# Attention with value products of three key tiles per visit, and each group's output projection added up by DVE in the next group

## The chip, the cores and the metric

The kernel runs on one core of a Trainium2 chip. The metric is device time in microseconds, the median of several executions. One execution was also recorded by the hardware profiler; the numbers of engines and single instructions come from it.

The engines have short names here: PE multiplies matrices (PEld is its loading of weights, which runs beside it), ACT computes functions such as the exponential, DVE and POOL work elementwise, SP issues most transfers (DMA). Each engine runs its own instructions in order. PE writes its results to PSUM, a memory of eight banks; a bank holds one result of 128x512 floats.

## The reference, cut to what matters

One sequence of 2048 tokens with 448 features goes through two branches, attention `a` and a mixer with a channel MLP `b`, and a gate `g` mixes them. The change concerns the attention alone: 16 heads of 28 features share one set of keys and values.

```python
q = (x @ wq).reshape(B, S, H, Dh).transpose(0, 2, 1, 3)     # S 2048, H 16, Dh 28
k = x @ wk
v = x @ wv
scores = einsum("bhqd,bkd->bhqk", q, k) * (Dh ** -0.5)
p = softmax(scores, axis=-1)
o = einsum("bhqk,bkd->bhqd", p, v)
a = o.transpose(0, 2, 1, 3).reshape(B, S, H * Dh) @ wo
...
return g * a + (1 - g) * b
```

## The kernel before

The first 424 us compute keys, values and the whole branch `b`, which ends in `x1`, 16 tiles of 128 tokens. The change leaves them alone. The attention stage follows, from line 454 on.

**Groups and key tiles.** Queries are taken in NB = 4 blocks of 512 tokens, heads in NG = 4 sets of four. A pair of a block and a set is a group `u`, 16 in all, and `b, g = divmod(u, 4)`. A group goes over 16 key tiles `kt` of 128 keys, so the main loop (line 646) counts `k` from 0 to 257, two steps (LAG) past the last of 256 key tiles.

**One step of the loop.** For each of four heads PE multiplies a key tile with 512 queries into a score tile `s` (L663), and ACT writes its exponential into a tile `p` (L665). Score tiles go round through five PSUM banks in order (`s_tile`, line 478): two of tag "mm", one of "misc", two of "s". The last group uses three of them; the "s" banks and both "m" banks then hold four output projections that stay open over the group.

**Visits.** At every PVB-th step (line 676) PE turns to value products: `pv_group` (line 618) multiplies the `p` tiles of a key tile with the values into the bank `pv` of the group (L625). With PVB = 2 a visit handles two key tiles, those of two and three steps before, 8 products of two instructions each. The four heads write four partition ranges of the bank and run side by side. The values carry a column of ones, so that row 0 of each range gets the softmax sums. Tag "mx" has one bank: the next group's `pv` takes it when the former has been copied.

**The end of a group.** After the last key tile `recip_begin` (line 523) copies `pv` to SBUF on ACT (`o`, L525), brings the sums into another layout by a transfer (`rt`), takes reciprocals on DVE and sends them back in two parts (`rb`). `norm_job` (line 541) spreads them with one matmul (`rbc`, L543), DVE multiplies, and POOL splits the result into a rounded part `onh` and a rest `onl`.

**Jobs.** Other matmuls are put between the scores. `jobs` is a list of generators, and `pump()` (line 601) runs one to its next yield, which is one matmul for the most part. It is called after the second and the fourth score of each step; in the last group after each. In the list come: `q_job(u + 2)` (from `kt` 2 on, 11 matmuls L503, then ACT and DVE split the result), the `norm_job` of the former group, and, once a block is complete, four `wo_job` (line 567), one for each tile of 128 tokens: 12 matmuls (L556, L558, L560) over the four sets of heads accumulate in one bank, `gate_out` scales them by the gate and adds `x1` on DVE (L564), and a transfer writes the tile out. The last block's sets 0 to 2 are done as jobs in the last group, the fourth in the tail.

**Maxima.** At the end of steps `kt` 6 to 9 four small matmuls (`m`, L166) and a reduction on DVE (L167) find row maxima for the next group; at `kt` 11 they are transposed (`mt`, L193) and copied by ACT (`mrow`, L195). The tiles `q`, `rbc`, `m`, `mt` and `wo` all share the two banks of tag "m". An instruction that wants a bank waits until its last reader is done, and on PE everything behind it waits too: PE's order is the order in which the code writes it.

**Tail.** After the loop the last group's result is transposed, divided, split and projected tile by tile (`tail_a`, `tail_b`, `tail_c`).

Of the kernel before, what the change touches and what calls it, by code (L numbers as in the profile page):

```python
# [8 lines left out]
F32 = mybir.dt.float32  # L9
F32R = mybir.dt.float32r  # L10
AF = mybir.ActivationFunctionType
ALU = mybir.AluOpType
# [3 lines left out]
P = 128  # L16
S = 2048
D = 448
# [4 lines left out]
NB = S // 512  # L23
NT = S // P
NF = F // P
NG = H // 4
# [1 line left out]
EPS = 1e-5  # L28
SHIFTS = (-1, 1, -2, 2)
LAG = 2  # L30
PVB = 2
MK = 128
LIMIT = 1e12

# [1 line left out]
def f32(ap):  # L36
    return ap.bitcast(F32)
# [3 lines left out]
def gated_mix_kernel(  # L41
# [13 lines left out]
    nc = tc.nc  # L55
# [11 lines left out]
    x1 = keep.tile([P, NT, D], F32, name="x1")  # L67
# [3 lines left out]
    gg = keep.tile([P, NT], F32, name="gg")  # L71
# [20 lines left out]
    def misc_tile(name):  # L92
        return psA.tile([P, 512], F32, tag="misc", bufs=1, name=name)
# [59 lines left out]
    NU = NB * NG  # L153
# [4 lines left out]
    def max_tile(name):  # L158
        return psA.tile([P, 512], F32, tag="mx", bufs=1, name=name)
# [294 lines left out]
    with tc.tile_pool(name="s3", bufs=1, reuse_waits="tile") as s3, \  # L454
# [8 lines left out]
        woh = s3.tile([P, 4, D], F32R, name="woh")  # L463
# [11 lines left out]
        def s_spare(name):  # L475
            return psA.tile([P, 512], F32, tag="misc", bufs=1, name=name)

        def s_tile(n, last=False):
            return (mm_tile, mm_tile, s_spare, s_more, s_more)[n % (3 if last else 5)](f"s_{n}")

        xact = {}

# [31 lines left out]
        on_of = {}  # L514
# [24 lines left out]
            return o, rb  # L539

        def norm_job(u, o, rb):
            ps = (mm_tile if u == NU - 2 else misc_tile)(f"rbc_{u}")
            nc.tensor.matmul(ps, sel8, rb, start=True, stop=True)  # L543
            on = s3.tile([P, 512], F32, tag="onf", bufs=2, name=f"on_{u}")
            nc.vector.tensor_mul(on, o, ps)  # L545
            onh = s3.tile([P, 512], F32R, tag="onh", bufs=5, name=f"onh_{u}")
            onl = s3.tile([P, 512], F32R, tag="onl", bufs=5, name=f"onl_{u}")
            nc.gpsimd.tensor_copy(onh, on)  # L548
            nc.gpsimd.tensor_tensor(onl, on, f32(onh), ALU.subtract)
            on_of[u] = (onh, onl)  # L550
            yield

        def wo_group(ps, b, t, g, first, last):
            tok = slice(t * P, (t + 1) * P)
            onh, onl = on_of[b * NG + g]
            nc.tensor.matmul(ps, onh[:, tok], woh[:, g, :], start=first, stop=False)  # L556
            yield
            nc.tensor.matmul(ps, onh[:, tok], wol[:, g, :], start=False, stop=False)  # L558
            yield
            nc.tensor.matmul(ps, onl[:, tok], woh[:, g, :], start=False, stop=last)  # L560

        def gate_out(n, ps):
            ot = s3.tile([P, D], F32, tag="ot", bufs=3, name=f"ot_{n}")
            nc.vector.scalar_tensor_tensor(ot, ps, gg[:, n:n + 1], x1[:, n, :], op0=ALU.mult, op1=ALU.add)  # L564
            nc.sync.dma_start(out[0, n * P:(n + 1) * P, :], ot)

        def wo_job(b, t):
            ps = misc_tile(f"wo_{b}_{t}")[:, 0:D]
            for g in range(NG):
                yield from wo_group(ps, b, t, g, g == 0, g == NG - 1)  # L570
                if g < NG - 1:
                    yield
            gate_out(4 * b + t, ps)
            yield

        wqraw = s3.tile([P, 4, 512], F32, tag="raw", bufs=2, name="wqraw")
        nc.sync.dma_start(wqraw, wq)
# [20 lines left out]
        jobs = []  # L598
# [13 lines left out]
        def drain():  # L612
            while current[0] is not None or jobs:
                pump()
# [3 lines left out]
        def pv_group(k):  # L618
            u, kt = divmod(k, NT)
            if kt == 0:  # L620
                pv_of[u] = max_tile(f"pv_{u}")
            pv = pv_of[u]
            ps = p_of.pop(k)
            for j in range(4):
                nc.tensor.matmul(pv[32 * j:32 * j + 32, :], vext[:, kt, :], ps[j],  # L625
                                 start=(kt == 0), stop=(kt == NT - 1), tile_position=(0, 32 * j))
            if kt == NT - 1 and u < NU - 1:
                o, rb = recip_begin(u, pv_of.pop(u))
                delayed.append((k + 6, lambda: norm_job(u, o, rb)))
                if u == NU - 2:  # L630
                    for t in range(4):
                        delayed.append((k + 10, lambda t=t: wo_last_job(t, NG - 2)))
                elif u % NG == NG - 1:
                    for t in range(4):
                        delayed.append((k + 8, lambda t=t: wo_job(u // NG, t)))

        wo_last = []

        def wo_last_job(t, g):
            if g == 0:  # L640
                wo_last.append((m_tile if t < 2 else s_more)(f"wo_{NB - 1}_{t}")[:, 0:D])
            yield from wo_group(wo_last[t], NB - 1, t, g, g == 0, False)
            yield

        delayed = []
        for k in range(NU * NT + LAG):
            u, kt = divmod(k, NT)
            while delayed and delayed[0][0] <= k:
                jobs.append(delayed.pop(0)[1])
            if k == (NU - 1) * NT:  # L650
                for g in range(NG - 2):
                    for t in range(4):
                        jobs.append(lambda t=t, g=g: wo_last_job(t, g))
            if k < NU * NT:
                if kt == (7 if u == 0 else 2) and u + 2 < NU:
                    jobs.insert(0, lambda u=u: q_job(u + 2))
                if kt == 8 and (u + 3) % NG == 0 and u + 3 < NU:
                    load_x((u + 3) // NG)
                p_of[k] = []
                for j in range(4):  # L660
                    n = 4 * k + j
                    ps = s_tile(n, u == NU - 1)
                    nc.tensor.matmul(ps, kS[0:98, kt * P:(kt + 1) * P], q_of[u][0:98, j, :], start=True, stop=True)  # L663
                    p = s3.tile([P, 512], F32, tag="p", bufs=4 * (LAG + PVB) + 2, name=f"p_{n}")
                    nc.scalar.activation(p, ps, AF.Exp, scale=SCALE)  # L665
                    p_of[k].append(p)
                    if j % 2 == 1 or u == NU - 1:
                        pump()
                if u + 1 < NU:
                    if 6 <= kt < 10:  # L670
                        max_part(u + 1, kt - 6, m_tile)
                    elif kt == 10:
                        max_end(u + 1)
                    elif kt == 11:
                        max_rows(u + 1, m_tile)
            if k >= LAG and k % PVB == PVB - 1:
                for kk in range(k - LAG - PVB + 1, k - LAG + 1):
                    if kk >= 0:
                        pv_group(kk)
        assert not delayed  # L680
        drain()

        u = NU - 1
        pv = pv_of.pop(u)
        o = s3.tile([P, 512], F32, tag="o", bufs=2, name=f"o_{u}")
        onh = s3.tile([P, 512], F32R, tag="onh", bufs=5, name=f"onh_{u}")
        onl = s3.tile([P, 512], F32R, tag="onl", bufs=5, name=f"onl_{u}")
        on_of[u] = (onh, onl)
        toks = [slice(t * P, (t + 1) * P) for t in range(4)]
        on4 = {}  # L690
# [15 lines left out]
            nc.vector.tensor_sub(onl[:, toks[t]], tq, f32(onh)[:, toks[t]])  # L706

        def tail_c(t):
            for _ in wo_group(wo_last[t], NB - 1, t, NG - 1, False, True):
                pass  # L710
            gate_out(4 * (NB - 1) + t, wo_last[t])

        for t in range(4):
            nc.scalar.copy(o[:, toks[t]], pv[:, toks[t]])
# [19 lines left out]
        with tc.If(again > 0):  # L734
            for b in range(NB):
                load_x(b)
                for g in range(NG):
                    u = b * NG + g
                    for _ in q_job(u):
                        pass  # L740
                    max_full(u, m_tile)
                    max_end(u)
                    max_rows(u, m_tile)
                    pv = max_tile(f"pv2_{u}")
                    for kt in range(NT):
# [10 lines left out]
                for t in range(4):  # L756
                    for _ in wo_job(b, t):
                        pass


_OUTS = [((1, S, D), "float32")]
# [48 lines left out]
```

## Time and profile before

| | us |
|---|---|
| median of three runs | 1070.64 (1069.9 to 1074.41) |
| the profiled execution | 1070.98 |
| its span, first to last instruction | 1069.1 |
| first score of the attention stage | 423.9 from the start |
| last group, first score | 1007.5 |
| span of the last value products | 1049.9 to 1053.6 |

The page of a profile lists, for each engine, busy time, share of the span and number of instructions, then the chain of work that ended last, then the costliest groups of instructions. A group's line gives the line of the kernel, engine, operation, what is written and read, the shapes, the count, then the busy time and the mean of one in ns, then idle time of the engine just before them and what ended most of it. Matmuls overlap, so the mean length of one is more than the distance between two.

### The profile page before, as it was taken

The numbers are of one execution on the slowest core, as the hardware profiler recorded it, in microseconds if no ns is written. First come the engines' busy times: TensorE is split into PE (matmuls) and PEld (weight loads), VectorE is DVE, ScalarE is ACT, GpSimd is POOL, SyncE is SP. The second block draws the span as 40 slices with busy tenths as digits, with TensorE's granted clock in tenths as the row PEclk, the third lists the DMA queues.
The fourth block names the chain that finished last, engine by engine and source line by source line (L and its number), as shares of the span: only waits on it lengthen the run. The fifth ranks groups of instructions, "written<-read, shape, count | busy, mean of one in ns | idle before, by whom it ended". The sixth has DMA issues, their size and how long they took to land.

```text
span 1069.1 us, 13948 instructions
## 1 busy us (share of the span) xinstructions
PE 1039.7 (97%) x5610; PEld 679.6 (64%) x5610; DVE 258.0 (24%) x521; ACT 673.2 (63%) x1318; POOL 159.8 (15%) x182
## 2 busy tenths in 40 slices
PE   6999889999999999999999999999999999999995
PEld 4787778888888888454554555554655555555542
DVE  6744952311411311401110110120110210111102
ACT  5444451222222223788888888889888889888873
POOL 5622430110200201603000002010002100000100
PEclk9999899999999999999999999999999999999998
DMA  9401330000000000423211202220202220211001
GB/s 312 131 1 37 111 111 1 1 1 1 1 1 1 1 1 29 164 32 70 33 17 16 31 20 40 39 31 3 39 10 41 39 31 2 40 24 26 10 2 38
DMA packets 30541, 41.15 MB, mean 38 GB/s; under 512 B 8004, under 2 KB 20100, under 8 KB 30340
## 3 DMA queue, kind: packets, MB, share of 16 engines
q1 hardware_dynamic: 30324, 40.04, 16.3%
q8 instruction: 46, 0.75, 0.3%
q14 instruction: 27, 0.22, 0.1%
q10 hardware_dynamic: 144, 0.13, 0.1%
HBM read 23.28 MB, written 3.67 MB: 25 GB/s over the span
## 4 chain that ended last, share of the span: by engine, by line
PE 91%; DVE 4%; DMA 1%; ACT 1%; POOL 1%; issue 1%; SPq 0%; POOLq 0%; ACTq 0%; DVEq 0%
PE s L663 27%; PE pv L625 22%; PE acc L420 4%; PE acc L419 4%; PE acc L421 4%; PE g L115 4%; PE g L116 4%; PE g L117 4%; PE q L503 3%; PE m L166 2%; PE wo L560 1%; PE wo L558 1%; PE wo L556 1%; PE g L119 1%; PE g L118 1%; PE h L116 1%
## 5 line engine op out<-in xcount | busy, mean ns | idle before, releaser
L665 ACT ACTIVATE p<-s 128x512 f32<-128x512 f32 x1024 | 517.6, 627 | 98.1 <-PE s L663 97.8
L663 PE MATMUL s<-qs,kS 98*128 98x512 f32 x1024 | 343.6, 420 | 1.4 <-ACT p L665 0.7
L663 PEld LDWEIGHTS s<-qs,kS 98*128 98x128 f32 x1024 | 181.6, 189 | 168.2 <-ACT p L665 127.1
L625 PE MATMUL pv<-p,vext 128*32 128x512 f32 x2048 | 247.6, 602 | 0.0
L409 ACT ACTIVATE gh<-g 128x512 fp32r<-128x512 f32 x56 | 33.6, 600 | 174.9 <-PE g L119 174.9
L625 PEld LDWEIGHTS pv<-p,vext 128*32 128x32 f32 x2048 | 53.7, 109 | 107.6 <-issue 100.3
L411 DVE TENSOR_TENSOR gl<-gf,gh 128x512 fp32r<-128x512 f32 x56 | 41.3, 738 | 192.1 <-ACT gf L410 192.0
L419 PE MATMUL acc<-w4h,gh 128*128 128x448 f32 x224 | 82.6, 369 | 0.0
L420 PE MATMUL acc<-w4l,gh 128*128 128x448 f32 x224 | 82.0, 366 | 0.0
L421 PE MATMUL acc<-w4h,gl 128*128 128x448 f32 x224 | 81.7, 365 | 0.0
L167 DVE TENSOR_REDUCE mr<-m 128x4 f32<-128x512 f32 x64 | 44.3, 692 | 146.0 <-PE m L166 145.3
L548 POOL CAST onh<-on 128x512 fp32r<-128x512 f32 x15 | 9.2, 614 | 414.8 <-DVE on L545 228.7
L115 PE MATMUL g<-ah,w3h 128*128 128x512 f32 x168 | 67.1, 399 | 3.1 <-ACT gf L410 2.8
L116 PE MATMUL g<-al,w3h 128*128 128x512 f32 x168 | 66.5, 396 | 0.1
L117 PE MATMUL g<-ah,w3l 128*128 128x512 f32 x168 | 66.3, 394 | 0.0
L521 DVE SCALAR_TENSOR_TENSOR good<-rt,good 128x16 f32<-128x16 f32 x15 | 2.6, 175 | 190.2 <-DMA rt<-o 190.2
L419 PEld LDWEIGHTS acc<-w4h,gh 128*128 128x128 f32 x224 | 42.0, 188 | 4.9
L420 PEld LDWEIGHTS acc<-w4l,gh 128*128 128x128 f32 x224 | 42.1, 188 | 4.8
L421 PEld LDWEIGHTS acc<-w4h,gl 128*128 128x128 f32 x224 | 42.0, 188 | 3.6
L166 PEld LDWEIGHTS m<-kS,qs 96*128 96x128 f32 x256 | 38.4, 191 | 6.3 <-DVE mr L167 1.2
L115 PEld LDWEIGHTS g<-ah,w3h 128*128 128x128 f32 x168 | 31.9, 190 | 9.7 <-ACT gf L410 3.3
L564 DVE SCALAR_TENSOR_TENSOR ot<-wo,gg,x 128x448 f32<-128x448 f32 x16 | 10.9, 682 | 108.0 <-PE wo L560 108.0
(204 smaller groups left out, 1144.4 us busy)
## 6 DMA issues: line engine op xcount, KB each, us to landing
qs<-qh SPq DMA_DIRECT2D x32, 256.0 KB
qs<-ql SPq DMA_DIRECT2D x16, 256.0 KB
xq<-in_xT_dram SPq DMA_DIRECT2D x4, 1024.0 KB
x<-in_x_dram SPq DMA_DIRECT2D x4, 896.0 KB
w3raw<-in_w_dram SPq DMA_DIRECT2D x7, 512.0 KB
out_dram<-ot SPq DMA_DIRECT2D x16, 224.0 KB
w4raw<-in_w_dram SPq DMA_DIRECT2D x7, 448.0 KB
xkv<-in_xT_dram SPq DMA_DIRECT2D x3, 1024.0 KB
```

Source lines behind the costliest of these rows:

```text
L115: nc.tensor.matmul(ps, wh[:, c, :], ah[:, c, :], start=(c == 0), stop=False)
L116: nc.tensor.matmul(ps, wh[:, c, :], al[:, c, :], start=False, stop=False)
L117: nc.tensor.matmul(ps, wl[:, c, :], ah[:, c, :], start=False, stop=False)
L166: nc.tensor.matmul(ps[:, j, :], q_of[u][0:96, j, t * P:(t + 1) * P], kS[0:96, 0:MK], start=True, stop=True)
L167: nc.vector.reduce_max(mx_of[u][:, :, t], ps, axis=AX.X)
L411: nc.vector.tensor_sub(gl, gf, f32(gh))
L419: nc.tensor.matmul(ps, gh[:, tok], w4h[i][:, k, :], start=(f == 0), stop=False)
L420: nc.tensor.matmul(ps, gh[:, tok], w4l[i][:, k, :], start=False, stop=False)
L421: nc.tensor.matmul(ps, gl[:, tok], w4h[i][:, k, :], start=False, stop=(f == NF - 1))
L625: nc.tensor.matmul(pv[32 * j:32 * j + 32, :], vext[:, kt, :], ps[j], start=(kt == 0), stop=(kt == NT - 1), tile_position=(0, 32 * j))
L663: nc.tensor.matmul(ps, kS[0:98, kt * P:(kt + 1) * P], q_of[u][0:98, j, :], start=True, stop=True)
L665: nc.scalar.activation(p, ps, AF.Exp, scale=SCALE)
```

## The change

A visit handles three key tiles (PVB = 3). Score tiles rotate through five banks in the last group too. `pump()` is called at six of the twelve scores between two visits, the 5th, 7th, 8th, 10th, 11th and 12th. `norm_job` no longer goes through the list of jobs, but runs at `kt` 7 of the next group as a whole. At `kt` 9 four `wo_job` of that former group join the list: three matmuls each in a bank of their own, and DVE adds the scaled result to `x1` (for the first set of heads) or to the sum so far in `ot` (for the others). After the fourth set the tile is written out. `onh` and `onl` have two buffers instead of five, `ot` five instead of three, and `p` has 22 instead of 18, since the count follows PVB.

```diff
-PVB = 2
+PVB = 3
...
-        def s_tile(n, last=False):
-            return (mm_tile, mm_tile, s_spare, s_more, s_more)[n % (3 if last else 5)](f"s_{n}")
+        def s_tile(n):
+            return (mm_tile, mm_tile, s_spare, s_more, s_more)[n % 5](f"s_{n}")
...
         def norm_job(u, o, rb):
-            ps = (mm_tile if u == NU - 2 else misc_tile)(f"rbc_{u}")
+            ps = misc_tile(f"rbc_{u}")
...
-        def wo_job(b, t):
-            ps = misc_tile(f"wo_{b}_{t}")[:, 0:D]
-            for g in range(NG):
-                yield from wo_group(ps, b, t, g, g == 0, g == NG - 1)
-                if g < NG - 1:
-                    yield
-            gate_out(4 * b + t, ps)
-            yield
+        ot_of = {}
+
+        def wo_job(u, t, tile_of=misc_tile):
+            b, g = divmod(u, NG)
+            n = 4 * b + t
             tok = slice(t * P, (t + 1) * P)
+            onh, onl = on_of[u]
+            ps = tile_of(f"wo_{u}_{t}")[:, 0:D]
+            nc.tensor.matmul(ps, onh[:, tok], woh[:, g, :], start=True, stop=False)
             yield
             nc.tensor.matmul(ps, onh[:, tok], wol[:, g, :], start=False, stop=False)
             yield
+            nc.tensor.matmul(ps, onl[:, tok], woh[:, g, :], start=False, stop=True)
+            before = x1[:, n, :] if g == 0 else ot_of[n]
+            if g == 0:
+                ot_of[n] = s3.tile([P, D], F32, tag="ot", bufs=5, name=f"ot_{n}")
+            nc.vector.scalar_tensor_tensor(ot_of[n], ps, gg[:, n:n + 1], before, op0=ALU.mult, op1=ALU.add)
+            if g == NG - 1:
+                nc.sync.dma_start(out[0, n * P:(n + 1) * P, :], ot_of[n])
...
                 o, rb = recip_begin(u, pv_of.pop(u))
-                delayed.append((k + 6, lambda: norm_job(u, o, rb)))
-                if u == NU - 2:
-                    for t in range(4):
-                        delayed.append((k + 10, lambda t=t: wo_last_job(t, NG - 2)))
-                elif u % NG == NG - 1:
-                    for t in range(4):
-                        delayed.append((k + 8, lambda t=t: wo_job(u // NG, t)))
+                norms.append((u, o, rb))
...
         for k in range(NU * NT + LAG):
             u, kt = divmod(k, NT)
-            while delayed and delayed[0][0] <= k:
-                jobs.append(delayed.pop(0)[1])
-            if k == (NU - 1) * NT:
-                for g in range(NG - 2):
-                    for t in range(4):
-                        jobs.append(lambda t=t, g=g: wo_last_job(t, g))
+            if norms and kt == 7:
+                for _ in norm_job(*norms[0]):
+                    pass
+            if norms and kt == 9:
+                v = norms.pop()[0]
+                for t in range(4):
+                    jobs.append(lambda t=t, v=v: wo_job(v, t))
...
-                    if j % 2 == 1 or u == NU - 1:
+                    if 4 * (k % PVB) + j in (4, 6, 7, 9, 10, 11):
                         pump()
...
         def tail_c(t):
-            for _ in wo_group(wo_last[t], NB - 1, t, NG - 1, False, True):
+            for _ in wo_job(u, t, m_tile if t < 2 else s_more):
                 pass
-            gate_out(4 * (NB - 1) + t, wo_last[t])
```

A branch behind the tail, which recomputes the attention if a softmax sum was too large, calls the changed functions in the same order; it did not run in the profiled execution.

More of the change, by code (lines that the diff above doesn't have):

```diff
@@ L545, in norm_job @@
             nc.vector.tensor_mul(on, o, ps)
-            onh = s3.tile([P, 512], F32R, tag="onh", bufs=5, name=f"onh_{u}")
-            onl = s3.tile([P, 512], F32R, tag="onl", bufs=5, name=f"onl_{u}")
+            onh = s3.tile([P, 512], F32R, tag="onh", bufs=2, name=f"onh_{u}")
+            onl = s3.tile([P, 512], F32R, tag="onl", bufs=2, name=f"onl_{u}")
             nc.gpsimd.tensor_copy(onh, on)
@@ L551, in norm_job @@
             yield
-        def wo_group(ps, b, t, g, first, last):
+        ot_of = {}
+        def wo_job(u, t, tile_of=misc_tile):
+            b, g = divmod(u, NG)
+            n = 4 * b + t
             tok = slice(t * P, (t + 1) * P)
-            onh, onl = on_of[b * NG + g]
-            nc.tensor.matmul(ps, onh[:, tok], woh[:, g, :], start=first, stop=False)
+            onh, onl = on_of[u]
+            ps = tile_of(f"wo_{u}_{t}")[:, 0:D]
+            nc.tensor.matmul(ps, onh[:, tok], woh[:, g, :], start=True, stop=False)
             yield
@@ L559, in wo_group @@
             yield
[L560 to L565, printed above, removed]
-        def wo_job(b, t):
-            ps = misc_tile(f"wo_{b}_{t}")[:, 0:D]
-            for g in range(NG):
-                yield from wo_group(ps, b, t, g, g == 0, g == NG - 1)
-                if g < NG - 1:
-                    yield
-            gate_out(4 * b + t, ps)
-            yield
+            nc.tensor.matmul(ps, onl[:, tok], woh[:, g, :], start=False, stop=True)
[5 more added lines that the diff above has]
+                nc.sync.dma_start(out[0, n * P:(n + 1) * P, :], ot_of[n])
         wqraw = s3.tile([P, 4, 512], F32, tag="raw", bufs=2, name="wqraw")
@@ L628, in pv_group @@
                 o, rb = recip_begin(u, pv_of.pop(u))
-                delayed.append((k + 6, lambda: norm_job(u, o, rb)))
-                if u == NU - 2:
-                    for t in range(4):
-                        delayed.append((k + 10, lambda t=t: wo_last_job(t, NG - 2)))
-                elif u % NG == NG - 1:
-                    for t in range(4):
-                        delayed.append((k + 8, lambda t=t: wo_job(u // NG, t)))
[L637 to L645, printed above, removed]
+                norms.append((u, o, rb))
+        norms = []
         for k in range(NU * NT + LAG):
             u, kt = divmod(k, NT)
-            while delayed and delayed[0][0] <= k:
-                jobs.append(delayed.pop(0)[1])
-            if k == (NU - 1) * NT:
-                for g in range(NG - 2):
-                    for t in range(4):
-                        jobs.append(lambda t=t, g=g: wo_last_job(t, g))
+            if norms and kt == 7:
[5 more added lines that the diff above has]
+                    jobs.append(lambda t=t, v=v: wo_job(v, t))
             if k < NU * NT:
@@ L661, in gated_mix_kernel @@
                     n = 4 * k + j
-                    ps = s_tile(n, u == NU - 1)
+                    ps = s_tile(n)
                     nc.tensor.matmul(ps, kS[0:98, kt * P:(kt + 1) * P], q_of[u][0:98, j, :], start=True, stop=True)
@@ L679, in gated_mix_kernel @@
                         pv_group(kk)
-        assert not delayed
+        assert not norms
         drain()
@@ L685, in gated_mix_kernel @@
         o = s3.tile([P, 512], F32, tag="o", bufs=2, name=f"o_{u}")
-        onh = s3.tile([P, 512], F32R, tag="onh", bufs=5, name=f"onh_{u}")
-        onl = s3.tile([P, 512], F32R, tag="onl", bufs=5, name=f"onl_{u}")
+        onh = s3.tile([P, 512], F32R, tag="onh", bufs=2, name=f"onh_{u}")
+        onl = s3.tile([P, 512], F32R, tag="onl", bufs=2, name=f"onl_{u}")
         on_of[u] = (onh, onl)
@@ L755, in gated_mix_kernel @@
                         pass
-                for t in range(4):
-                    for _ in wo_job(b, t):
-                        pass
+                    for t in range(4):
+                        for _ in wo_job(u, t):
+                            pass
 _OUTS = [((1, S, D), "float32")]
```

## The prediction

> **What bounds the kernel now.** I read the page first: engine times, the chain that ended last, the groups of instructions.
>
> ```profile
> PE 1039.7 (97%) x5610; PEld 679.6 (64%) x5610; DVE 258.0 (24%) x521; ACT 673.2 (63%) x1318; POOL 159.8 (15%) x182
> ...
> PE 91%; DVE 4%; DMA 1%; ACT 1%; POOL 1%; issue 1%; SPq 0%; POOLq 0%; ACTq 0%; DVEq 0%
> ...
> L665 ACT ACTIVATE p<-s 128x512 f32<-128x512 f32 x1024 | 517.6, 627 | 98.1 <-PE s L663 97.8
> ...
> L564 DVE SCALAR_TENSOR_TENSOR ot<-wo,gg,x 128x448 f32<-128x448 f32 x16 | 10.9, 682 | 108.0 <-PE wo L560 108.0
> ```
>
> PE looks full, but that is busy time. The waits, between 462 and 1054 us, say otherwise:
>
> ```profile
> PEld s L663 <- ACT p L665: 118.9, 220, 0.8
> ```
>
> So score matmuls wait on the exponentials, and L665 shows the exponentials waiting on scores: the two run in a loop through the five score banks. Its clockwork is in the timeline. The columns are start, time from the first start to the last end, engine, line, what is written and read, count, idle time before. First a visit with no extra matmuls (all engines; PE, then ACT), then one with four:
>
> ```profile
> 733.87 2.67 PE L663 MATMUL s<-qs,kS 98*128 98x512 f32 x8
> 736.47 1.92 PE L625 MATMUL pv<-p,vext 128*32 128x512 f32 x16
> 738.32 0.73 PE L663 MATMUL s<-qs,kS 98*128 98x512 f32 x2
> ...
> 734.41 4.03 ACT L665 ACTIVATE p<-s 128x512 f32<-128x512 f32 x8 [0.42 <-PE s L663]
> ...
> 735.38 0.60 ACT L665 ACTIVATE p<-s 128x512 f32<-128x512 f32 x1
> ...
> 736.04 0.50 PE L663 MATMUL s<-qs,kS 98*128 98x512 f32 x1
> ```
>
> ```profile
> 703.34 1.92 PE L625 MATMUL pv<-p,vext 128*32 128x512 f32 x16
> 705.19 0.73 PE L663 MATMUL s<-qs,kS 98*128 98x512 f32 x2
> 705.76 0.40 PE L503 MATMUL q<-alq,wqh 128*128 128x512 f32 x1
> 706.00 0.63 PE L663 MATMUL s<-qs,kS 98*128 98x512 f32 x2
> 706.47 0.39 PE L503 MATMUL q<-ahq,wql 128*128 128x512 f32 x1
> ...
> 707.88 0.39 PE L503 MATMUL q<-alq,wqh 128*128 128x512 f32 x1
> 708.20 1.92 PE L625 MATMUL pv<-p,vext 128*32 128x512 f32 x16
> ```
>
> In the plain visit the first score starts at 733.87 and its exponential 0.54 later. The third exponential ends at 735.98, 1.57 after the first began; the eighth score, which needs its bank, starts at 736.04 (+0.06); the value products start 0.43 later and the next score 1.85 after them. 0.54 + 1.57 + 0.06 + 0.43 + 1.85 = 4.45 us: **a loop through the banks**, in which PE and ACT both wait. In the loaded visit PE streams, one matmul every 0.236 us (705.76 to 706.47 holds three); it lasts 4.86 us (703.34 to 708.20). The first score after value products takes 0.335 (0.57 less 0.235), the step into them 0.32, and the way from them to the next score is 1.85, 0.13 over four steps of 0.43 (below): 0.10 + 0.085 + 0.13, one switch costs about 0.31 us.
>
> The bank loop can be tested inside this trace. In the last group scores rotate through three banks, so the eighth waits for the fifth exponential, 2 x 0.49 later (eight end 4.03 after the first starts, three 1.57: 0.49 each). The loop gives 4.45 + 0.98 = 5.43; the chain of waits shows 5.43 from value products to value products, and in the timeline ACT idles 1.41 instead of 0.42:
>
> ```profile
> 1022.14 1.85 PE pv L625 x16
> 1027.57 1.85 PE pv L625 x16
> ```
>
> ```profile
> 1041.44 4.03 ACT L665 ACTIVATE p<-s 128x512 f32<-128x512 f32 x8 [1.41 <-PE s L663]
> ```
>
> **Part 1: three key tiles per visit.** It removes 43 of 129 visits: 43 x 0.31 = 13.3 us if PE alone decided. The Trainium skill says the same in "TensorEngine Tiling (Array Packing)", Tiling Modes, Key Properties: changing the tiling mode drains the TensorE, so fewer changes are fewer drains. The row agrees that a change costs; by this rule alone the kernel gains, and that is a rival below.
>
> But banks stay five while a visit has twelve scores, so the twelfth waits for the *seventh* exponential, which ends 1.57 + 4 x 0.49 = 3.54 after the first begins. The value products are 24 instructions. Their pace:
>
> ```profile
> 1007.54 0.50 PE L663 MATMUL s<-qs,kS 98*128 98x512 f32 x1
> ...
> 1049.91 3.64 PE L625 MATMUL pv<-p,vext 128*32 128x512 f32 x32
> ```
>
> 32 less 16 of them is 3.64 - 1.92 = 1.72 us, 0.43 for each four; so 1.85 + 0.86 = 2.71 to the next score. A plain visit: 0.54 + 3.54 + 0.06 + 0.43 + 2.71 = **7.28 us for three tiles, 2.43 a tile against 2.22**. Five exponentials cover about 2.4 us and no longer reach over the value products: ACT idles some 1.5 us a visit. "Perfetto Trace Analysis", Optimization Strategy, in the Trainium skill, reads a bubble that repeats as a buffer that ran out; the trace agrees, with 1.41 us a visit on three banks.
>
> With all six pump slots filled: the tenth score waits for the fifth exponential, to 0.54 + 2.55 + 0.06 = 3.15; then 0.335, four steps of 0.235 and 0.32 to the value products, 4.75; + 2.71 = 7.46 (PE without waits: 0.335 + 16 x 0.235 + 0.32 + 2.71 = 7.13). That is 2.49 a tile against 2.43.
>
> **Part 2: what falls into a visit's chain.** A group needs 11 q and 12 wo matmuls, in 32 slots. Three groups (48 tiles) are 16 visits; by the slots, ten have a filled last slot: 16 x 7.28 + 10 x 0.18 = 118.3 us. Then:
>
> ```profile
> 711.57 0.56 PE L166 MATMUL m<-kS,qs 96*128 96x128 f32 x4
> ...
> 713.17 0.56 PE L166 MATMUL m<-kS,qs 96*128 96x128 f32 x4
> 713.66 1.92 PE L625 MATMUL pv<-p,vext 128*32 128x512 f32 x16
> ...
> 712.16 0.69 DVE L167 TENSOR_REDUCE mr<-m 128x4 f32<-128x512 f32 x1 [8.40 <-PE m L166]
> ```
>
> The m matmuls at the end of a visit add about 0.4 (0.49 to the value products instead of 0.32, and a step of 0.235), four times in three groups, 1.6; the others, rbc and mt with ACT's mrow mostly hide in bank waits, 1.0 (from 0 if all hide to 2.5 if none). 2.6 together.
>
> **Part 3: the value bank, a new wait.** The tag "mx" has one bank. Sixteen is not a multiple of three, so a visit now holds the last key tile of one group *and* the first of the next in two of three groups (u mod 3 = 0 and 2); the next group's first product must wait for ACT's copy o, and behind it wait all later value products and scores. Before, this boundary fell between visits:
>
> ```profile
> 698.47 1.92 PE L625 MATMUL pv<-p,vext 128*32 128x512 f32 x16
> ...
> 700.46 0.59 ACT L525 COPY o<-pv 128x512 f32<-128x512 f32 x1
> ```
>
> For u mod 3 = 0 the old group's products end 1.92 into the visit, the copy follows 0.07 later and takes 0.59, products resume at about 2.64 instead of 1.72: 0.9. For u mod 3 = 2 the old products end at 1.06, but ACT first finishes its queued exponentials (twelve, 0.48 apart from 0.54 on, to 6.3; the products begin at 4.75), so the copy runs from 1.55 to 2.14; resumed at 2.2 instead of 0.86: 1.3. With 0.2 for the third group's copy, 2.4 per three groups. Bounds: 0 if ACT takes the copy early, 3.4 if every boundary also sees a full copy after idle.
>
> **Part 4: norm_job at kt 7.** It leaves the job queue and asks at once for one of two "m" banks. In groups with u mod 3 = 0 and 1 the pump slots leave q at nine matmuls by then, so q holds one and the m of kt 6 the other. rbc waits for that reduction: m at 711.57, reduction from 712.16 to 712.85, so 1.33 us after m's start instead of 0.40, and every later score of the visit queues behind. By the steps above the twelfth score comes 1.1 and 1.3 late: 2.4 per three groups; nothing if q is done earlier. Where u mod 3 = 2, q is done. The copy lies a whole visit, over 7 us, ahead of rbc; I take rb's small transfers as landed by then.
>
> **Part 5: projections and DVE.** The 192 matmuls stay; 48 more additions of 0.68 us (L564) are 33 us on a DVE that is busy 24%: nothing on the path, except that an "m" bank is held 0.7 us after each wo_job, under the steps to the next (0.1 if not). Output transfers stay 16; with five ot buffers the fifth is free 38 us ahead. p has 22 buffers for 20 live ones, the margin of two as before.
>
> **Sum.** Three groups: 118.3 + 2.6 + 2.4 + 2.4 = 125.7, 41.9 a group. Before, by the copies:
>
> ```profile
> L525 ACT COPY o<-pv x15: 587/587/588, 468.1 to 1013.1; 128x512 f32<-128x512 f32 x15
> ```
>
> (1013.1 - 468.1) / 14 = 38.9. Fourteen groups: +41.6, less 0.6 because u = 14 computes no q. **The last group gains**: five banks, and no saved-up projections. It ran from 1007.54 to 1053.55, 46.0 us. After: three visits of 7.28, two of 7.46, 0.9 for the value bank, then four scores (1.12) and 24 products (2.78): 41.6, so -4.4. The first group and the tail (the same three matmuls and one addition for each t) I take as unchanged. +36.6 in all. The profiled execution took 1071.0 us (span 1069.1), 0.3 above the median of 1070.64; forecast **1108 us**, 3.5% slower.
>
> **The rivals.**
> *The new waits stay away* (parts 3 and 4 cost nothing). For it: the order of ACT's queue isn't in the diff, and a q finished by kt 6 frees its bank. Against: one "mx" bank, two "m" banks. Ten boundaries cost 11.0 and nine norm jobs 11.0: without them 1108 - 22 = 1086 us.
> *The switches decide, faster.* If PE's own stream sets each visit, 43 switches of 0.31 are saved, 13.3, and 4.4 in the last group: 1070.6 - 17.7 = 1053 us. For it: PE at 97%, and loaded visits stream without a wait. Against: the 5.43 us loop of the last group. It decides from the point where a visit's bank chain is about half a microsecond shorter than I have it (37 us over 75 visits); exponentials near 0.41 us apart would do that. The skill's drain rule gives this result, taken alone.
> *The clock drops.* Longer waits on PE at three places in a group could lower its granted clock, as happened once at the start of this stage, where scores ran at ACT's pace:
>
> ```profile
> 424.00:463.60 39.60, 39.11 (x206) 18.82 (x204) 12.50 (x16) 32.57 (x66) 21.75 (x16) 0.96 0.53 150
> 463.60:615.00 151.40, 151.40 (x889) 79.02 (x888) 21.23 (x49) 131.37 (x266) 14.28 (x11) 1.00 0.18 30
> ```
>
> (Busy times of the engines, then the granted clock: 0.96, later 1.00.) 0.04 of 40 us is 1.6; if every second group lost that, and the waits of parts 3 and 4 were half as long again (11), 1108 + 12 + 11 = 1131 us. Against: later waits of up to 0.8 us left it at 1.00.
>
> **Chances.** Forecast 0.65, waits stay away 0.18, switches decide 0.10, clock 0.07. The forecast's own range is 1098 to 1118: part 2's hidden work (5 units of three groups by -1.0 to +1.5) and a few us in the last group. The range 1082 to 1122 takes in the first rival and leaves out the others. Within 0.5%, about what a measurement of this kernel can tell from no change, needs gains and waits to cancel: 0.02. Faster 0.10, slower 0.88.
>
> **What would show it.** Plain visits of 7.28 and loaded ones of 7.46 between starts of value products; ACT idle about 1.5 us before the first exponential of each. Value products waiting on ACT's o at ten boundaries, 0.9 and 1.3 us. rbc waiting on DVE's reduction in nine groups, over 1 us. A last group near 41.6. Visits near 7.1 with no score waiting on p would prove part 1 wrong, and with it the sign.

## The result and the profile after

| | before | changed |
|---|---|---|
| median | 1072.28 us (four runs) | 1117.1 us (1115.56 to 1120.57, four runs) |
| ratio | 1 | 1.0429, interval 1.0407 to 1.0450 |
| profiled execution | 1070.98 us, span 1069.1 | 1118.51 us, span 1116.6 |

The change makes the kernel 4.3% slower. By busy time PE still looks full on the page (96%, 97 before). But PE's share of the chain that ended last has fallen from 91 to 85%, and ACT's has risen from 1 to 5%.

```profile
PE 1072.1 (96%) x5610; PEld 671.7 (60%) x5610; DVE 289.0 (26%) x569; ACT 669.7 (60%) x1318; POOL 159.3 (14%) x182
...
PE 85%; ACT 5%; DVE 5%; POOL 1%; DMA 1%; issue 1%; SPq 0%; ACTq 0%; POOLq 0%
...
L649 ACT ACTIVATE p<-s 128x512 f32<-128x512 f32 x1024 | 514.7, 643 | 147.6 <-PE s L647 147.6
```

The same 1024 exponentials now wait 147.6 us for scores, 98.1 before. PE's waits in the attention stage, between 463 and 1103 us, name what else is new (who waited for whom: total, times, longest):

```profile
PE pv L622 <- ACT o L525: 9.8, 10, 1.4
PE rbc L543 <- DVE mr L167: 7.1, 9, 0.8
PE m L166 <- DVE ql L148: 1.3, 4, 0.3
```

Ten value products wait for the copy of the former group, nine `rbc` for a reduction: the counts that the prediction gave. Two visits without a job, PE and then ACT in the timeline (start, time from first start to last end, engine, line, what is written and read, count, idle time before):

```profile
498.58 2.78 PE L622 MATMUL pv<-p,vext 128*32 128x512 f32 x24
501.29 4.63 PE L647 MATMUL s<-qs,kS 98*128 98x512 f32 x12
505.85 2.78 PE L622 MATMUL pv<-p,vext 128*32 128x512 f32 x24
...
501.83 5.99 ACT L649 ACTIVATE p<-s 128x512 f32<-128x512 f32 x12 [1.53 <-PE s L647]
```

From value products to value products 7.27 us (7.28 predicted), and ACT sits idle for 1.53 before the first exponential. Next, the two kinds of boundary between two groups that fall inside a visit (first u mod 3 = 0, with ACT's copy, then u mod 3 = 2), and a visit in which `rbc` finds both "m" banks taken:

```profile
552.98 1.92 PE L622 MATMUL pv<-p,vext 128*32 128x512 f32 x16
555.61 1.07 PE L622 MATMUL pv<-p,vext 128*32 128x512 f32 x8 [0.70 <-ACT o L525]
...
554.97 0.59 ACT L525 COPY o<-pv 128x512 f32<-128x512 f32 x1 [0.26 <-PE pv L622]
...
769.26 1.06 PE L622 MATMUL pv<-p,vext 128*32 128x512 f32 x8
771.53 1.92 PE L622 MATMUL pv<-p,vext 128*32 128x512 f32 x16 [1.21 <-ACT o L525]
```

```profile
565.20 0.56 PE L166 MATMUL m<-kS,qs 96*128 96x128 f32 x4
566.54 0.50 PE L543 MATMUL rbc<-rb,sel 128*128 128x512 f32 x1 [0.79 <-DVE mr L167]
...
570.15 0.66 PE L166 MATMUL m<-kS,qs 96*128 96x128 f32 x4 [0.34 <-DVE ql L148]
```

In the first the new group's eight products start 2.63 us after the visit's first instead of 1.72: 0.91 late (0.9 predicted). In the second its sixteen start 2.27 after instead of 0.86: 1.41 late (1.3 predicted). `rbc` starts 1.34 after the m matmuls (1.33 predicted). In the last row the third m of that visit waits too, since the bank that q held is not split yet; this one was not predicted.

### The profile page after: what moved, and what is told of

Same layout as the page of the kernel before. It is cut to its first block, busy times and chain, and to the rows that moved or that the text cites. A ratio compares the mean times of both kernels' runs of the same rounds, so it can differ in the third digit from the quotient of the medians.

```text
span 1116.6 us, 14066 instructions
## 1 busy us (share of the span) xinstructions
PE 1072.1 (96%) x5610; PEld 671.7 (60%) x5610; DVE 289.0 (26%) x569; ACT 669.7 (60%) x1318; POOL 159.3 (14%) x182
## 4 chain that ended last, share of the span: by engine, by line
PE 85%; ACT 5%; DVE 5%; POOL 1%; DMA 1%; issue 1%; SPq 0%; ACTq 0%; POOLq 0%
PE s L647 25%; PE pv L622 21%; ACT p L649 4%; PE acc L420 4%; PE acc L419 4%; PE acc L421 4%; PE g L115 3%; PE g L116 3%; PE g L117 3%; PE q L503 3%; PE m L166 2%; PE wo L561 1%; PE g L119 1%; PE g L118 1%; PE wo L565 1%; PE wo L563 1%
## 5 line engine op out<-in xcount | busy, mean ns | idle before, releaser
L649 ACT ACTIVATE p<-s 128x512 f32<-128x512 f32 x1024 | 514.7, 643 | 147.6 <-PE s L647 147.6
L647 PE MATMUL s<-qs,kS 98*128 98x512 f32 x1024 | 368.0, 432 | 0.5
L647 PEld LDWEIGHTS s<-qs,kS 98*128 98x128 f32 x1024 | 184.8, 188 | 181.9 <-ACT p L649 109.1
L622 PEld LDWEIGHTS pv<-p,vext 128*32 128x32 f32 x2048 | 58.0, 111 | 141.3 <-issue 118.7
L569 DVE SCALAR_TENSOR_TENSOR ot<-wo,gg,ot 128x448 f32<-128x448 f32 x48 | 32.7, 683 | 107.0 <-PE wo L565 107.0
L166 PE MATMUL m<-kS,qs 96*128 96x128 f32 x256 | 36.4, 264 | 1.8 <-DVE ql L148 1.3
```

The lines of the kernel that those rows point to most:

```text
L166: nc.tensor.matmul(ps[:, j, :], q_of[u][0:96, j, t * P:(t + 1) * P], kS[0:96, 0:MK], start=True, stop=True)
```

## The experiments

**Four score banks, without and with a second bank for value products.** The chain through the banks was read out of one trace; with one bank less it should get longer by one exponential.

```diff
 def s_more(name):
-    return ps3.tile([P, 512], F32, tag="s", bufs=2, name=name)
+    return ps3.tile([P, 512], F32, tag="s", bufs=1, name=name)
...
-    return (mm_tile, mm_tile, s_spare, s_more, s_more)[n % 5](f"s_{n}")
+    return (mm_tile, mm_tile, s_spare, s_more)[n % 4](f"s_{n}")
```

> The changed kernel with four score banks instead of five. My theory: the twelfth score waits for the eighth exponential instead of the seventh, 0.49 us later: plain visits of 7.76 us instead of 7.27, some 0.5 us in about 66 of 85 visits (the ones with rbc or with all m matmuls hide some of it): about 1150 us. Rival (visits are set by PE's own stream and its switches): within 4 us of the changed kernel's 1117.

1157.8 us, ratio to the kernel before 1.0792 (1.0768 to 1.0817). A visit without a job, in the timeline of this kernel:

```profile
598.07 2.78 PE L622 MATMUL pv<-p,vext 128*32 128x512 f32 x24
600.78 5.12 PE L647 MATMUL s<-qs,kS 98*128 98x512 f32 x12
605.82 0.64 PE L622 MATMUL pv<-p,vext 128*32 128x512 f32 x4
```

7.75 us, 7.76 expected. One bank less costs one exponential more in a visit without a job; the rival that PE's own stream sets the visit is out. (In all 41 us were lost, not 33. Three groups without a spell of lower clock take 133.08 us, from 697.55 to 830.63, where the changed kernel takes 126.55: about 35 us over 86 visits, so the longer loop shows through in more visits than I had counted. The trace also has five such spells, which are the subject of "The clock" below, against three in the changed kernel's.)

```diff
-                pv_of[u] = max_tile(f"pv_{u}")
+                pv_of[u] = max_tile(f"pv_{u}") if u % 2 else ps3.tile([P, 512], F32, tag="pv", bufs=1, name=f"pv_{u}")
```

> As with four score banks, and the bank that is set free holds the value products of every second group, so that no group waits for the copy of the former. My theory: ten waits on o of 0.9 to 1.1 us go, 1140 us, 10 us less than with four banks alone. Rival (the copy's wait lies beside exponentials that have to be done anyway): the same as with four banks alone, within 3 us.

1152.9 us, 5 less than with four banks alone; neither 10 nor 0. The waits themselves went altogether: with four banks alone the list of waits has ten, in this kernel it has no such line.

```profile
PE pv L622 <- ACT o L525: 7.0, 10, 0.7
```

Visits with such a boundary got shorter by it: 9.13 us with four banks alone (522.25 to 531.38), 8.15 here (519.33 to 527.48), which over ten boundaries makes about 10 us. The clock took part of it back: the trace's record of the granted clock has eight spells of 3.4 us at half speed after 460 us, against five with four banks alone, and one costs up to 1.7 us. So the value bank's wait is on the path. Its worth, measured on four banks alone, is 5 us in time; about 10 without the clock is an estimate from these visits.

**norm_job one step earlier.**

```diff
-            if norms and kt == 7:
+            if norms and kt == (7 if u % 3 == 2 else 6):
```

> The changed kernel with norm_job at kt 6 instead of 7 in groups with u mod 3 = 0 and 1, ahead of that step's m matmuls, so that the matmul bank it asks for is free. My theory: rbc's wait on DVE's reduction (7.1 us of PE in nine waits in the trace) goes, the visits of 9.0 and 9.3 us become 7.7 to 8.1, 1.2 us in each of nine groups: about 1106 us. Rival (the wait only moves to the m matmuls behind it, or these visits are held by ACT): 1115 us or more.

1106.95 us (1105.99 to 1108.71), ratio 1.0322 (1.0302 to 1.0341). The line of `rbc` is gone from the waits, the ten of value products stay at 9.8 us. This wait was worth 10 us.

**Each half of the change alone.** First the projections group by group, with two tiles per visit:

```diff
-PVB = 3
+PVB = 2
...
-                    if 4 * (k % PVB) + j in (4, 6, 7, 9, 10, 11):
+                    if j % 2 == 1:
```

> The changed kernel with two key tiles per visit again and pumps after the second and fourth score of a step; projections stay group by group with DVE adding up. My theory (the loss comes from the three-tile visits: seven instead of three exponentials in a visit's chain, and the value bank): visits of 4.45 us plain and 4.86 loaded come back, value products wait on no copy of o; what stays is the wait of rbc at kt 7, about 1.2 us in each group, so a normal group takes about 40.5 us against 38.9 before, the last about 39.5 against 46.0: 1087 us, at most 1095. Rival (the projection part, with 48 more additions and its use of the matmul banks, carries the loss): it stays at 1110 us or more.

1079.53 us (1078.65 to 1081.83), ratio 1.0070 (1.0050 to 1.0090): 38 of the 45 us are gone with the third tile. It came out 7 us better than I expected, as a group takes 39.9 us and not 40.5, and the last 38.3 and not 39.5. `rbc` waits here in nearly every group:

```profile
PE rbc L543 <- DVE mr L167: 10.2, 13, 0.8
```

Then three tiles per visit in the kernel before:

```diff
-PVB = 2
+PVB = 3
...
-            on = s3.tile([P, 512], F32, tag="onf", bufs=2, name=f"on_{u}")
+            on = s3.tile([P, 512], F32, tag="onf", bufs=1, name=f"on_{u}")
...
-            ot = s3.tile([P, D], F32, tag="ot", bufs=3, name=f"ot_{n}")
+            ot = s3.tile([P, D], F32, tag="ot", bufs=2, name=f"ot_{n}")
...
-                    p = s3.tile([P, 512], F32, tag="p", bufs=4 * (LAG + PVB) + 2, name=f"p_{n}")
+                    p = s3.tile([P, 512], F32, tag="p", bufs=4 * (LAG + PVB), name=f"p_{n}")
```

> The kernel before with three key tiles per visit and nothing else of the change (p has 20 buffers, just the live ones, and one buffer each of onf and ot is taken away so that it fits). My theory: plain visits of 7.28 us, loaded ones of 7.5, ten waits of value products on o, the last group on three score banks at 8.3 to 8.5 us a visit, 48 to 49 us: 41.3 us a normal group, about 1108 us. Rival (three tiles per visit save switches, and the projection part is what costs): 1075 us or less.

1117.6 us (1112.55 to 1118.3), ratio 1.0428 (1.0399 to 1.0457): 9 to 10 us more than expected, but the same loss as the whole change. The copies and the waits:

```profile
L525 ACT COPY o<-pv x15: 585/586/727, 469.9 to 1054.7; 128x512 f32<-128x512 f32 x15
...
PE pv L625 <- ACT o L525: 9.6, 10, 1.2
...
PE rbc L543 <- DVE ql L148: 2.9, 5, 0.7
```

(1054.7 - 469.9) / 14 = 41.8 us a group, and 48.7 for the last, on three banks (a spell of lower clock costs 1.2 of it). The profiled execution was the fastest of the five. Plain visits take 7.26 us, so the smaller number of `p` buffers does not show in them. Three tiles alone cost as much as the whole change. That does not make the projection half free: by the copies of the changed kernel, from 469.3 to 1067.2, its groups take 42.7 us, 0.9 longer than here (three spells and the waits of `rbc` are in them), and its last group 41.6, 7 shorter. The two about cancel.

**Projections group by group in the last block only**, in the kernel before:

```diff
-                if u == NU - 2:
+                if u >= NU - NG:
                     for t in range(4):
-                        delayed.append((k + 10, lambda t=t: wo_last_job(t, NG - 2)))
+                        delayed.append((k + 8, lambda t=t: wo_last_job(t, u)))
...
+            ps = tile_of(f"wo_{u}_{t}")[:, 0:D]
+            yield from wo_group(ps, b, t, g, True, True)
+            before = x1[:, n, :] if g == 0 else ot_of[n]
...
+            nc.vector.scalar_tensor_tensor(ot_of[n], ps, gg[:, n:n + 1], before, op0=ALU.mult, op1=ALU.add)
...
-                    ps = s_tile(n, u == NU - 1)
+                    ps = s_tile(n)
```

> The kernel before, two tiles per visit, where only the last block of queries has its projections group by group, added up by DVE, so that the last group keeps five score banks. Theory: this half of the change is what the last group gained: its 46.0 us become 39 to 40, two groups ahead of it get 12 more matmuls and about 1 us each; 1066 us, ratio 0.996. Rival (the matmuls moved into the two groups and the additions eat it up): 1071 us, ratio 1.000.

1068.25 us (1065.25 to 1069.06), ratio 0.9959 (0.9945 to 0.9974); the last group takes 40.0 us instead of 46.0. (The edit also leaves out the extra pumps of the last group, and gives `onf` one buffer instead of two and `ot` four instead of three.) The gain that the prediction gave to five banks in the last group is real, and can be had without three tiles.

**The clock.** Now and then a visit of the changed kernel is stretched. One starts at 632 us; the windows of the trace around it and around a second (length, busy times of PE, PEld, DVE, ACT and POOL, granted clock, share of DMA, GB/s):

```profile
632.41 4.48 PE L622 MATMUL pv<-p,vext 128*32 128x512 f32 x24
```

```profile
440.00:620.00 180.00, 175.30 (x1010) 90.06 (x1008) 33.83 (x69) 141.99 (x288) 22.16 (x15) 1.00 0.23 45
620.00:640.00 20.00, 19.90 (x96) 8.97 (x92) 1.36 (x2) 14.65 (x31) 0.00 (x0) 0.91 0.07 25
640.00:880.00 240.00, 231.48 (x1322) 118.02 (x1323) 46.58 (x95) 186.81 (x380) 24.61 (x18) 1.00 0.16 25
880.00:900.00 20.00, 18.81 (x95) 7.66 (x98) 0.69 (x1) 15.23 (x31) 0.00 (x0) 0.91 0.01 2
```

4.48 us for products that take 2.78. A mean clock of 0.91 over 20 us is 3.6 us at half speed; the trace's record of the granted clock has a spell of 3.4. It happens three times after 460 us in this execution (at 632, 888 and 977 us), each time right behind a visit without a job. So these visits were given something to do:

```diff
                     if 4 * (k % PVB) + j in (4, 6, 7, 9, 10, 11):
+                        if current[0] is None and not jobs and j < 3 and (kt < 2 or kt >= 12):
+                            ps = misc_tile(f"fill_{n}")
+                            nc.tensor.matmul(ps, kS[0:98, 0:P], kS[0:98, 0:512], start=True, stop=True)
                         pump()
```

> The changed kernel with one matmul of 512 columns, read by nobody, at each empty pump slot of the steps kt 0, 1 and 12 to 15 where the next matmul is a score; the output stays the reference's. Theory on the 9 us that the prediction missed: about 5 us are three spells of 3.4 us at half the granted clock, in visits with no job, where PE waits for exponentials for a fifth of the time; with the waits filled the spells after 440 us go, and the fillers cost nothing, since they lie in these waits: ratio of the changed kernel to this one 1.003 to 1.005, about 1112 us. Rival (the spells come whatever PE does, or the fillers lengthen the visits): 1117 us or more.

1115.1 us (1113.47 to 1117.07), ratio to before 1.0404 (1.0380 to 1.0428). The profile of this kernel has no spell in these windows, nor elsewhere after 460 us (one at 442 stays, in the first group, as one at 434 in the changed kernel), and a visit with four fillers lasts as long as one with none, 7.26 us:

```profile
620.00:640.00 20.00, 19.91 (x114) 9.84 (x106) 1.37 (x2) 15.37 (x32) 0.00 (x0) 1.00 0.10 36
640.00:880.00 240.00, 231.50 (x1343) 120.51 (x1343) 46.58 (x95) 186.77 (x380) 24.57 (x18) 1.00 0.16 25
880.00:900.00 20.00, 18.80 (x111) 8.23 (x111) 1.29 (x5) 14.67 (x31) 0.00 (x0) 1.00 0.01 2
```

```profile
626.14 2.78 PE L622 MATMUL pv<-p,vext 128*32 128x512 f32 x24
...
633.40 2.78 PE L622 MATMUL pv<-p,vext 128*32 128x512 f32 x24
```

In these two traces the theory holds: four matmuls cost nothing where PE waits, and the spans are 1112.6 against 1116.6 us. The medians differ by 2 us with intervals that overlap, so the gain in time is not settled: the changed kernel has executions with few spells too (two of its four took 1115.6 us at a mean clock of 0.986 to 0.987, the others 1118.5 and 1120.6 at 0.982 and 0.981; the six with fillers ran at 0.985 to 0.987).

**Two tiles, with the banks looked after.** If three tiles and `rbc` are the loss, the projection half should beat the kernel before once both are mended. `PVB = 2`, pumps after the second and fourth score, `norm_job` at `kt` 6:

> The changed kernel with two key tiles per visit, pumps after the second and fourth score, and norm_job at kt 6. Theory: with two tiles a visit the projections group by group cost a normal group 40.0 us only because of rbc's wait (10.2 us of PE in 13 waits); without it the visit with rbc takes 5.7 instead of 6.7 us: 39.0 us a group, last group 38.3: about 1065 us, ratio 0.993, faster than before. Rival (two tiles cost as much with either place of norm_job, since the m matmuls then wait): 1079 us, ratio 1.007.

1066.51 us (1064.23 to 1068.01), ratio 0.9947 (0.9927 to 0.9966). 39.0 us a group, as expected. The same with three slots in each visit:

```diff
-                    if j % 2 == 1:
+                    if 4 * (k % PVB) + j in (4, 6, 7):
```

> The same with three pump slots in each visit (after the fifth, seventh and eighth score) instead of four in most and none in two. Theory: a visit of two tiles has room for two extra matmuls beside the bank loop (4.45 us against 3.92 of PE's own), so spreading 24 over eight visits fills what two visits leave empty: 38.4 to 38.6 us a group, about 1058 to 1061 us, ratio 0.988. Rival (q, finished only at kt 9, holds a matmul bank and the m matmuls queue for the other; or wo_job spills past the end): 1066 us or more.

1070.42 us, ratio 0.9988 (0.9975 to 1.0001): the expectation failed, a group took 39.3. A visit of it:

```profile
581.81 0.45 PE L647 MATMUL s<-qs,kS 98*128 98x512 f32 x1
582.11 0.37 PE L565 MATMUL wo<-woh,onl 128*128 128x448 f32 x1
582.41 1.92 PE L622 MATMUL pv<-p,vext 128*32 128x512 f32 x16
```

The eighth score, which had to wait for its bank, is followed by 0.30 to the job and 0.30 to the value products: a matmul behind the last score lies beside nothing. Such a visit takes 4.65 us (582.41 to 587.06). Moved ahead, `(4, 5, 6)`:

> Two tiles per visit, norm_job at kt 6, three pump slots per visit after the fifth, sixth and seventh score, none behind the eighth. Theory on why three slots gained nothing: a matmul behind the eighth score comes after the wait on the third exponential and adds 0.2 us to the bank loop, in each of eight visits; moved ahead of that wait it lies beside it, visits of 4.65 us become 4.54 to 4.62 and a group 38.5 instead of 39.25: about 1060 us, ratio 0.989. Rival (the slots do not matter, the visit is full): 1068 us or more.

```profile
577.49 0.37 PE L565 MATMUL wo<-woh,onl 128*128 128x448 f32 x1
577.69 0.39 PE L647 MATMUL s<-qs,kS 98*128 98x512 f32 x1
578.01 1.92 PE L622 MATMUL pv<-p,vext 128*32 128x512 f32 x16
...
582.55 0.64 PE L622 MATMUL pv<-p,vext 128*32 128x512 f32 x4
```

Visits of 4.54 us (578.01 to 582.55), 1060.31 us (1058.14 to 1061.94), ratio 0.9890 (0.9873 to 0.9907): the fastest version of this study, 1.1% faster than the kernel before, on the projection half of the change.

**One tile per visit**, in the version with `norm_job` at `kt` 6, to weigh the switches alone (`PVB = 1`):

> The same as with norm_job at kt 6, but one key tile per visit, so that the five banks always cover it and only the number of switches grows (128 more). Theory: PE alone sets the pace, a switch costs 0.31 us as read from the trace of before: some 41 us a group, 1097 us. Rival (a switch is hidden behind ACT, so that the premise of the faster rival was empty): 1066 us.

1090.4 us, ratio 1.0175 (1.0147 to 1.0203), 40.7 us a group by the copies. Against 39.0 with two tiles, eight more switches a group cost 1.7 us net. The visits show what that is made of; first two with a job in every slot, then two without jobs:

```profile
555.24 1.06 PE L622 MATMUL pv<-p,vext 128*32 128x512 f32 x8
...
557.83 1.07 PE L622 MATMUL pv<-p,vext 128*32 128x512 f32 x8
...
586.70 1.07 PE L622 MATMUL pv<-p,vext 128*32 128x512 f32 x8
587.70 1.20 PE L647 MATMUL s<-qs,kS 98*128 98x512 f32 x4
588.82 1.07 PE L622 MATMUL pv<-p,vext 128*32 128x512 f32 x8
```

With jobs a visit of one tile takes 2.59 us; two of them are 0.32 longer than the 4.86 of a loaded two-tile visit, the price of the switch (0.31 in the prediction). Without jobs it takes 2.12, and two of them are 0.21 *shorter* than the 4.45 of a plain two-tile visit. So fewer switches save time only where jobs fill PE's stream. Where they do not, the banks take back more: a key tile without jobs costs 2.12, 2.22 and 2.42 us in visits of one, two and three tiles.

## Why the prediction was right, and what it missed

The forecast was 1108 us, 36.6 more than before; measured were 1117.1, 44.8 more. The sign and the mechanism held, and the size was 8 us short. That 1117.1 still lies within the forecast's own range, 1098 to 1118, is in part luck: two of the four executions lie above it, and the range had been drawn for part 2 and the last group, while the clock took a share too.

*Part 1* held to the hundredth: 7.27 us plain for 7.28. Visits with all six slots filled take 7.47 with `wo` (707.66 to 715.13), as the 7.46 of the prediction, and 7.60 with `q` (722.39 to 729.99). The four-bank run moves the plain visit as the formula says, and the PVB halves show that three tiles are the bulk of the loss. The faster rival is out; its premise, that a switch costs time, is right where jobs fill PE.

*Part 3* held: ten waits, 0.91 us for 0.9 and 1.41 for 1.3.

*Part 4* held: nine waits, 1.34 for 1.33, and 10 us by experiment for 11.0. The first rival (both waits stay away) is out.

*The last group* took 41.6 us as predicted. Its reason, five banks and no saved-up projections, is borne out by the run of the last block only.

The profiled span grew by 47.5 us, 10.9 more than forecast. This shortfall lies in the size of three terms of the sum. **The clock** was put into a rival of its own with a chance of 0.07 and left out of the forecast, against "later waits of up to 0.8 us left it at 1.00". Three visits with a spell, such as 9.19 us from 632.41 to 641.60 where its like takes 7.60, make 5 us of the profiled execution. In time it may be less: the two executions with a clock like that of the kernel before, 0.986 to 0.987, are 3 us shorter than the profiled one, and at 1115.6 still 7.6 above the forecast (of which 1.6 is the kernel before, at 1072.28 instead of 1070.64). The longest wait was the wrong measure, as I read it: with the steps of the prediction PE's own stream in a plain visit is 0.335 + 10 x 0.235 + 0.32 + 2.71 = 5.72 us of 7.27, so PE is idle for a fifth of the time, 0.30 us at once. The counts of spells in the loop after 460 us in the profiled executions fit that: none in any kernel with two tiles per visit (PE's stream 3.92 of 4.45, 12% idle), one to three with three tiles, five and eight with four banks (26%), none with the fillers. That the value bank's longer waits bring them is ruled out by the eight, in a kernel without these waits. No run gives the share at which it starts.

**Part 2** gave too little to m, q and their copies: 118.3 + 2.6 + 2.4 + 2.4 = 125.7 us for three groups, while two boundaries of that kind without a spell between them are 126.55 apart (first two rows). With `norm_job` a step earlier they are 124.16 apart (last two, of that kernel):

```profile
682.37 1.92 PE L622 MATMUL pv<-p,vext 128*32 128x512 f32 x16
...
808.92 1.92 PE L622 MATMUL pv<-p,vext 128*32 128x512 f32 x16
...
804.46 1.92 PE L622 MATMUL pv<-p,vext 128*32 128x512 f32 x16
...
928.62 1.92 PE L622 MATMUL pv<-p,vext 128*32 128x512 f32 x16
```

So `rbc` is worth 2.39 for the 2.4 of part 4, and the value bank's 0.91 and 1.41 are nearly the 2.4 of part 3; what is missing, 0.85 in three groups and 4 us over fourteen, is left to part 2. The m that waits for `ql` and the 7.60 of visits filled with `q` are part of it. **Part 5** overlooked POOL's queue. In one group the split of the next block's input, loaded at `kt` 8, sits ahead of `onh`, and the projections, now due at `kt` 9, wait for it; that visit took 9.22 us (650.73 to 659.95), 1.1 longer than its like:

```profile
650.21 1.89 POOL L488 CAST ahq<-xq 128x2048 fp32r<-128x2048 f32 x1 [39.44 <-PE q L503]
652.18 3.50 POOL L489 TENSOR_TENSOR alq<-xq,ahq 128x1536 fp32r<-128x1536 f32 x1
655.76 1.28 POOL L490 TENSOR_TENSOR ahq<-xq,ahq 64x512 fp32r<-64x512 f32 x1
657.11 0.61 POOL L548 CAST onh<-on 128x512 fp32r<-128x512 f32 x1
```

5 + 4 + 1 is about what is missing in the profiled execution. The first group, which the sum took as unchanged though it has visits of three tiles too, was 1.2 us longer (its copy starts at 469.3, before at 468.1), and the tail 1.2 us shorter, for which I have no reason.

## What to carry to other kernels

Where one engine fills buffers and another empties them, count how long the full buffers last against the longest thing that the filling engine does in between. Here five banks cover about 2.4 us; value products of one tile (1.00 us to the next score) leave a visit at PE's own pace, those of two (1.85) make a key tile without jobs 0.1 us longer than that, those of three (2.71) 0.3. Work that hides in such a wait hides only ahead of the instruction that waits: a visit of two tiles with three jobs took 4.65 us with the last one behind that instruction, 4.54 with all ahead of it. And a period that does not divide the loop (three in sixteen) moves buffers' ends into the middle of a burst.

## What the runs showed of the hardware

The granted clock fell without any long pause of PE. In the visit ahead of the spell at 632 us the weight loads of seven of the twelve scores wait for a bank, for 0.20 to 0.30 us each (the changed kernel's timeline, PEld; the five rows that follow are like the second):

```profile
629.04 0.19 PEld L647 LDWEIGHTS s<-qs,kS 98*128 98x128 f32 x1 [0.20 <-ACT p L649]
629.53 0.19 PEld L647 LDWEIGHTS s<-qs,kS 98*128 98x128 f32 x1 [0.30 <-ACT p L649]
```

In the changed kernel the spells of 3.4 us at half speed came behind such visits, though not behind each of them, and they were gone from the trace after 460 us when matmuls that nobody reads were put into these waits. "TensorE: Matmul & The Clock Gate", A second HAM failure mode: psum-queue depth-cycling, in the Trainium skill, describes, for a bf16 kernel, such small idle times between groups of matmuls that bring the throttle back; the traces agree, with 0.91 of the clock in the windows of the spells and 1.00 with the fillers.
